# A fused delta rule and rational MoE on one core: the second layer's products one unit later, with a fourth operand buffer

## The chip, the cores and the metric

The kernel runs on one core of one Trainium2 chip. The metric is device time in microseconds (us). Engines in the text: PE is TensorE's matmul, PEld its weight load, DVE is VectorE, ACT is ScalarE, POOL is GpSimd, SP the engine whose queue issues nearly all DMAs.

## What is computed

A delta-rule attention over 768 steps for 4 x 8 heads of size 48 makes 3072 tokens of 384 values; a layer of 2048 hidden values with a rational activation follows.

```
for t in range(S):                       # attention, state is D x D per head
    y[:, :, t] = q_t @ state
    state = state + bt * outer(kt, vt - state @ kt)
x = y as [3072, 384]
h = x @ w_in                             # 384 x 2048
P = a[0] + a[1]*h + a[2]*h*h + a[3]*h*h*h
Q = 1 + |b[0]|*|h| + |b[1]|*h*h
out = (P / (Q + 1e-6)) @ w_out           # 2048 x 384
```

## The kernel before

The sequence is cut into 12 chunks of 64 steps (256 tokens each, all batches together). For each chunk the attention part is a chain: key products (`pg`), an inverse on DVE, query products (`pm`), a triangular solve in passes (`pu`, with the residuals `z_0`, `z_1`, `z_2`, `z`), the next state (`pd`, `S`), and the outputs `y` (line 788). `tokens(c)` turns `y` of a chunk into the layer's operand `xT`: a matmul and a DVE reduction find a scale (L806, L807), six PE transposes read `y` (L819), ACT copies the scale `sf` (L812), and ACT and DVE split the result into two fp16 halves (L246, L250).

The layer works in units: chunk c has 8 units j, each of 256 hidden values, written c.j below; there are 96. A unit has four steps:

- `hidden`: 18 matmuls into `ph` (L851).
- `numerator`: ACT makes `mu` and `mr` from `ph` (L868, L870), DVE does L871, L873, L875, ACT takes the absolute value `mw` (L874).
- `quotient`: ACT takes Ln and Exp (L886, L887); DVE makes the high half of the operand `mg` (L890 or L892), then L893; DVE (L897) or, in 4 of 8 units of chunks 2 to 10, POOL (L895) subtracts, and POOL makes the low half of `mg` (L898).
- `accumulate`: 12 matmuls of `mg` with `w_out` into the two banks `po` (L913), 6 for each bank. `po` is one pair of banks: the first unit of a chunk can write it only when ACT has moved the chunk before it out into the tile `ob` (L927, two copies, one for each bank), which then goes to memory.

Tiles with one tag share a fixed number of buffers, in the order in which the program asks for them. `mg` (and, while the weights are loaded, `wa` of `to_f32`) has MB = 3 buffers, as have `mu`, `mr` and `mw`. `ob` has one buffer, and the chunk's `y` has the same tag:

```
y = ys[c] = sb.tile([P, NPAIR, DM], F32, tag="ob", name=f"y_{c}", bufs=1)
obs[c] = sb.tile([P, NPAIR, DM], F32, tag="ob", name=f"ob_{c}", bufs=1)
```

In iteration n the program asks for numerator(n), quotient(n-1), the attention steps of position n+2, accumulate(n-2) and hidden(n+1). In chunk c's turn the attention part runs `back(c+1)`: `outputs` (which makes y of chunk c+1) at position 4, `tokens` (which reads it) at position 6, so at n = 8c+2 and n = 8c+4. A scheduler in the build then fixes the order of the instructions of each engine; each engine runs its list in that order.

Of the kernel before, what the change touches and what calls it, by code (L numbers as in the profile page):

```python
# [10 lines left out]
F16 = mybir.dt.float16  # L11
F32 = mybir.dt.float32
# [26 lines left out]
def kernel(  # L39
# [12 lines left out]
    nc = tc.nc  # L52
# [3 lines left out]
    P = 128  # L56
# [11 lines left out]
    NG = NPAIR * NH  # L68
    TG = NPAIR * P
    MB = 3  # L70
    SHIFT = 2
    SHAPE = {
        "k": [P, NPAIR, 2, NH, 2, C, HG],
# [9 lines left out]
    sb = ctx.enter_context(tc.tile_pool(name="sb", bufs=2))  # L83
# [282 lines left out]

    STAGES = (("mw", MB), ("mu", MB), ("mr", MB))
    stage = [0]

    def staged(shape, dtype, nm):  # L370
        stage[0] += 1
        tag, bufs = STAGES[stage[0] % len(STAGES)]
        return sb.tile(shape, dtype, tag=tag, name=nm, bufs=bufs)
# [4 lines left out]
    def to_f32(t, src, nm, keep=MIN_NORMAL):  # L378

        n = t.shape[-1]  # L380
        st = staged([P, n, 2], U32, "ws" + nm)
        nc.sync.dma_start(out=st.rearrange("p f w -> p (f w)"), in_=src)
        wl, wh = st[..., 0], st[..., 1]
        a = sb.tile([P, n], F32, tag="mg", name="wa" + nm, bufs=MB)
        nc.scalar.activation(a, wh.bitcast(F32), AF.Abs)
        nc.gpsimd.tensor_scalar(a, a, 3.0e38, keep, op0=ALU.min, op1=ALU.max)
        nc.vector.tensor_scalar(
            t, a.bitcast(U32), 3, KEEP, op0=ALU.logical_shift_left, op1=ALU.bitwise_and
        )
        for word, scalar, in1, op0, op1 in (  # L390
            (wh, 0xC0000000, t, ALU.bitwise_and, ALU.bitwise_or),
            (wl, 29, t, ALU.logical_shift_right, ALU.bitwise_or),
        ):
            nc.vector.scalar_tensor_tensor(out=t, in0=word, scalar=scalar, in1=in1, op0=op0, op1=op1)  # L394
# [428 lines left out]
    def scalars(c, lo, hi):  # L823

        d = toks[c]
        u = slice(lo, hi)
        sf = d["sf"]
        if c == 0:
            sf = sb.tile([P, 6], F32, tag="sf", name=f"sf_{c}_{lo}", bufs=3)
            pl = ps_h.tile([P, 6], F32, tag="h", name=f"pl_{c}_{lo}")  # L830
            looked_up(pl, d["hot"], t_x[:, int(lo > 0)])
            nc.scalar.copy(sf, pl)
        if lo == 0:
            d["m"] = sb.tile([P, 6, NU], F32, tag="msc", name=f"msc_{c}")
        nc.vector.tensor_mul(d["m"][:, :, u], tab[:, :, u], sf.unsqueeze(2).broadcast_to([P, 6, hi - lo]))
        d["ikap"][lo] = hi, sf[:, 1:2]
# [6 lines left out]
    def hidden(n):  # L843
        c, f2 = divmod(n, NU)
        x = toks[c]["x"]
        ph = ps_h.tile([P, 2, TG], F32, tag="h", name=f"ph_{n}")
        for i in range(2):
            k = 0
            for cc in range(NCC):
                for wp, xp in PASSES:  # L850
                    nc.tensor.matmul(  # L851
                        ph[:, i],
                        w_in[:, f2, wp, cc, i * P : (i + 1) * P],
                        x[:, xp, cc],
                        start=k == 0,
                        stop=k == 3 * NCC - 1,
                    )
                    k += 1
        unit[n] = {"ph": ph}

    def numerator(n):

        c, f2 = divmod(n, NU)
        d = unit[n]
        A3, B1, A1, B0, A0, Q0 = (toks[c]["m"][:, i, f2 : f2 + 1] for i in range(6))
        ph = d.pop("ph")
        u = sb.tile([P, 2, TG], F32, tag="mu", name=f"mu{n}", bufs=MB)
        nc.scalar.activation(u, ph, AF.Identity, scale=A3, bias=a2)  # L868
        r = z = sb.tile([P, 2, TG], F32, tag="mr", name=f"mr{n}", bufs=MB)
        nc.scalar.activation(z, ph, AF.Abs, scale=B1)  # L870
        nc.vector.tensor_mul(u, ph, u)  # L871
        w = sb.tile([P, 2, TG], F32, tag="mw", name=f"mw{n}", bufs=MB)
        nc.vector.scalar_tensor_tensor(out=w, in0=z, scalar=B0, in1=ph, op0=ALU.add, op1=ALU.mult)  # L873
        nc.scalar.activation(w, w, AF.Abs)  # L874
        nc.vector.scalar_tensor_tensor(out=u, in0=u, scalar=A1, in1=ph, op0=ALU.add, op1=ALU.mult)  # L875

        by_pool = 2 <= c < NCH - 1 and f2 in (0, 4, 5, 6)
        if by_pool:
            nc.gpsimd.tensor_scalar(u, u, A0, 1.0, op0=ALU.add, op1=ALU.mult)  # L879
        d.update(u=u, w=w, r=r, A0=A0, Q0=Q0, by_pool=by_pool)  # L880

    def quotient(n):

        d = unit[n]
        u, w, r, A0, Q0, by_pool = (d.pop(x) for x in ("u", "w", "r", "A0", "Q0", "by_pool"))
        nc.scalar.activation(r, w, AF.Ln, bias=Q0)  # L886
        nc.scalar.activation(r, r, AF.Exp, scale=-1.0)  # L887
        g = sb.tile([P, 2, 2, TG], F16, tag="mg", name=f"mg{n}", bufs=MB)
        if by_pool:
            nc.vector.tensor_mul(g[:, 0], u, r)  # L890
        else:
            nc.vector.scalar_tensor_tensor(out=g[:, 0], in0=u, scalar=A0, in1=r, op0=ALU.add, op1=ALU.mult)  # L892
        nc.vector.scalar_tensor_tensor(out=w, in0=w, scalar=Q0, in1=g[:, 0], op0=ALU.add, op1=ALU.mult)  # L893
        if by_pool:
            nc.gpsimd.tensor_sub(u, u, w)  # L895
        else:
            nc.vector.scalar_tensor_tensor(out=u, in0=u, scalar=A0, in1=w, op0=ALU.add, op1=ALU.subtract)  # L897
        nc.gpsimd.tensor_mul(g[:, 1], u, r)  # L898
        d["g"] = g

    def accumulate(n):
        c, f2 = divmod(n, NU)
        g = unit.pop(n)["g"]
        lo = max(i for i in toks[c]["ikap"] if i <= f2)
        hi, ikap = toks[c]["ikap"][lo]
        if f2 == lo:
            acc[c] = [ps_o.tile([P, DM], F32, tag=f"o{p}", name=f"po_{c}_{lo}_{p}") for p in PAIRS]
        po = acc[c]

        for k, (gp, wp) in enumerate(sorted(PASSES)):  # L910
            for i in range(2):
                for p in PAIRS:
                    nc.tensor.matmul(  # L913
                        po[p],
                        g[:, gp, i, p * P : (p + 1) * P],
                        w_out[:, f2, wp, i],
                        start=f2 == lo and i == 0 and k == 0,
                        stop=f2 == hi - 1 and i == 1 and k == len(PASSES) - 1,
                    )
        if f2 < hi - 1:  # L920
            return
        if lo == 0:
            obs[c] = sb.tile([P, NPAIR, DM], F32, tag="ob", name=f"ob_{c}", bufs=1)
        ob = obs[c]
        for p in PAIRS:
            if lo == 0:
                nc.scalar.activation(ob[:, p], po[p], AF.Copy, scale=ikap)  # L927
            else:
                nc.vector.scalar_tensor_tensor(
                    out=ob[:, p], in0=po[p], scalar=ikap, in1=ob[:, p], op0=ALU.mult, op1=ALU.add  # L930
                )
        if hi == NU:
            for b in range(2):
                dst = out[2 * b * S : (2 * b + 2) * S].rearrange("(p t) e -> t p e", p=NPAIR)
                nc.sync.dma_start(out=dst[c * C : (c + 1) * C], in_=ob[b * C : (b + 1) * C])
# [74 lines left out]
    def attention(c, j):  # L1010
        for f, cc in ((back, c + 1), (middle, c + 2), (front, c + 3), (ahead, c + 4)):
            if cc < NCH:
                f(cc, j)
# [16 lines left out]
    for what in ORDER:  # L1030
# [15 lines left out]
        f2 += what == "a"  # L1046
    for j in range(SHIFT):
        attention(0, j)
    N = NCH * NU
    hidden(0)  # L1050
    for n in range(N + 2):
        c, j = divmod(n, NU)
        if n < N:
            numerator(n)
        if 0 <= n - 1 < N:
            quotient(n - 1)
        attention(*divmod(n + SHIFT, NU))
        if 0 <= n - 2 < N:
            accumulate(n - 2)
        if n == GRP - 1 and GRP < NU:  # L1060
            tables(GRP, NU)
            scalars(0, GRP, NU)
        if n + 1 < N:
            hidden(n + 1)
# [26 lines left out]
```

## Time and profile before

| | |
|---|---|
| median of 3 runs | 855.29 us (854.32, 855.29, 863.12) |
| the profiled execution | 859.42 us, of it 857.2 us span |
| busy: DVE, PE, ACT, POOL | 760.8, 622.0, 544.9, 482.7 us |
| granted TensorE clock | 0.886 mean |

Busy time is a sum over the span. The span has three parts: weights are loaded until 147 us, attention and units run together until about 770 us, and the last chunk's units end it. Waits are told with the engine and tile that ended them.

### The profile page before, as it was taken

How to read it: one execution, taken by the hardware profiler on the slowest of the kernel's cores; microseconds unless marked ns; L12 is line 12 of the kernel's file. 1: busy time of each engine (PE TensorE's matmuls, PEld its weight loads, DVE VectorE, ACT ScalarE, POOL GpSimd, SP SyncE). 2: the span in 40 equal slices, each digit the busy share in tenths (PEclk: the TensorE clock that was granted, in tenths of full speed). 3: DMA queues.
4: the chain of work that ended last, by engine and by line, in shares of the span. 5: the costliest groups of instructions: out<-in, count | busy, mean ns of one | idle time of the engine just before them, and what ended most of it. 6: DMA issues, size and time to landing. Idle time of an engine off the chain costs nothing.

```text
span 857.2 us, 22995 instructions
## 1 busy us (share of the span) xinstructions
PE 622.0 (73%) x9290; PEld 492.0 (57%) x9290; DVE 760.8 (89%) x1312; ACT 544.9 (64%) x980; POOL 482.7 (56%) x452
## 2 busy tenths in 40 slices
PE   0220344766878688878798697995987989999895
PEld 0220344546666475666586585774775767777663
DVE  5998799697989969989989968999789999898996
ACT  4766656645666465677586574766566766677774
POOL 7655666355326437646736864766665635454532
PEclk9755555897988989989999899998989999999999
DMA  8996868898787875965997988598778672500000
GB/s 235 247 205 132 191 160 152 152 159 152 141 142 130 154 147 89 176 116 104 186 151 132 151 137 173 90 167 150 123 151 153 94 151 47 102 2 20 1 20 19
DMA packets 466506, 111.46 MB, mean 130 GB/s; under 512 B 431328, under 2 KB 463072, under 8 KB 466400
## 3 DMA queue, kind: packets, MB, share of 16 engines
q1 hardware_dynamic: 464224, 108.83, 67.8%
q8 instruction: 73, 1.20, 0.6%
q10 hardware_dynamic: 2176, 1.17, 0.5%
q14 instruction: 33, 0.27, 0.1%
HBM read 40.47 MB, written 26.23 MB: 78 GB/s over the span
## 4 chain that ended last, share of the span: by engine, by line
DVE 40%; DMA 16%; PE 14%; ACT 9%; issue 9%; SPq 7%; POOL 4%; POOLq 0%; ACTq 0%; DVEq 0%
PE ph L851 4%; PE po L913 4%; DVE mw L893 4%; DVE mw L873 3%; DVE mu L871 3%; DVE mg L892 3%; DVE mu L897 3%; DVE w_out L394 3%; DVE pr L636 2%; DVE mu L875 2%; DMA gd<-g 2%; DMA gb<-gd 2%; SPq L676 2%; POOL mg L898 2%; DMA wc<-img 1%
## 5 line engine op out<-in xcount | busy, mean ns | idle before, releaser
L913 PE MATMUL po<-w_out,mg 128*128 128x384 f16 x1152 | 224.9, 341 | 50.5 <-POOL mg L898 43.0
L851 PE MATMUL ph<-xT,w_in 128*128 128x256 f16 x1728 | 216.6, 278 | 13.1 <-DVE mu L875 11.4
L898 POOL TENSOR_TENSOR mg<-mu,mr 128x512 f16<-128x512 f32 x96 | 134.1, 1398 | 115.0 <-DVE mu L897 85.3
L851 PEld LDWEIGHTS <-w_in 128*128 128x128 f16 x1728 | 169.2, 100 | 45.5 <-issue 12.5
L913 PEld LDWEIGHTS <-mg 128*128 128x128 f16 x1152 | 110.2, 101 | 126.5 <-POOL mg L898 51.3
L868 ACT ACTIVATE mu<-ph,coef,msc 128x512 f32<-128x512 f32 x96 | 74.0, 771 | 45.5 <-POOL mg L898 31.0
L874 ACT ACTIVATE mw<-mw 128x512 f32<-128x512 f32 x96 | 60.3, 628 | 64.4 <-DVE mw L873 64.1
L893 DVE SCALAR_TENSOR_TENSOR mw<-mw,msc,mg 128x512 f32<-128x512 f32 x96 | 96.1, 1002 | 0.5
L470 PEld LDWEIGHTS <-kbd 128*128 128x128 f16 x1680 | 61.9, 105 | 36.4 <-issue 27.8
L871 DVE TENSOR_TENSOR mu<-ph,mu 128x512 f32<-128x512 f32 x96 | 65.4, 681 | 19.1 <-ACT mr L870 16.5
L875 DVE SCALAR_TENSOR_TENSOR mu<-mu,msc,ph 128x512 f32<-128x512 f32 x96 | 70.7, 736 | 0.0
L873 DVE SCALAR_TENSOR_TENSOR mw<-mr,msc,ph 128x512 f32<-128x512 f32 x96 | 70.5, 735 | 0.0
L886 ACT ACTIVATE mr<-mw,msc 128x512 f32<-128x512 f32 x96 | 69.2, 720 | 1.5
L895 POOL TENSOR_TENSOR mu<-mu,mw 128x512 f32<-128x512 f32 x36 | 48.7, 1353 | 32.8 <-DVE mw L893 29.1
L870 ACT ACTIVATE mr<-ph,msc 128x512 f32<-128x512 f32 x96 | 65.3, 680 | 0.0
L470 PE MATMUL pu<-z,ebd 128*128 128x48 f16 x1728 | 53.3, 187 | 15.7 <-DVE z L250 14.2
L470 PEld LDWEIGHTS <-ebd 128*128 128x128 f16 x1728 | 52.6, 99 | 19.5 <-issue 16.8
L887 ACT ACTIVATE mr<-mr 128x512 f32<-128x512 f32 x96 | 60.3, 628 | 1.4
L892 DVE SCALAR_TENSOR_TENSOR mg<-mu,msc,mr 128x512 f16<-128x512 f32 x60 | 56.9, 949 | 4.3 <-ACT mr L887 4.3
L879 POOL TENSOR_SCALAR mu<-mu,msc 128x512 f32<-128x512 f32 x36 | 34.2, 949 | 38.8 <-DVE mu L875 38.7
L897 DVE SCALAR_TENSOR_TENSOR mu<-mu,msc,mw 128x512 f32<-128x512 f32 x60 | 54.3, 907 | 0.4
L470 PEld LDWEIGHTS <-wbd 128*128 128x128 f16 x1152 | 35.1, 99 | 33.9 <-issue 30.4
(211 smaller groups left out, 1247.8 us busy)
## 6 DMA issues: line engine op xcount, KB each, us to landing
wsi<-in_moe_w_in_dram SPq DMA_DIRECT2D x24, 256.0 KB, 5.2
xdk<-kn SPq DMA_DIRECT2D x24, 256.0 KB, 3.9
kbd<-tk SPq DMA_DIRECT2D x24, 256.0 KB, 4.5
gd<-g SPq DMA_DIRECT2D x24, 256.0 KB, 4.3
wso<-in_moe_w_out_dram SPq DMA_DIRECT2D x32, 192.0 KB, 4.3
xdq<-kn SPq DMA_DIRECT2D x24, 256.0 KB, 4.3
mbd<-mm SPq DMA_DIRECT2D x24, 256.0 KB, 5.0
wc<-img SPq DMA_DIRECT2D x24, 256.0 KB, 5.1
```

What stands on the lines that cost most here:

```text
L470: nc.tensor.matmul(dst[p][:, h], head(bd, lp, p * H + h), head(rt, rp, p * H + h), start=start and n == 0 and h == 0, stop=stop and n == l ...
L851: nc.tensor.matmul(ph[:, i], w_in[:, f2, wp, cc, i * P : (i + 1) * P], x[:, xp, cc], start=k == 0, stop=k == 3 * NCC - 1,)
L868: nc.scalar.activation(u, ph, AF.Identity, scale=A3, bias=a2)
L871: nc.vector.tensor_mul(u, ph, u)
L873: nc.vector.scalar_tensor_tensor(out=w, in0=z, scalar=B0, in1=ph, op0=ALU.add, op1=ALU.mult)
L875: nc.vector.scalar_tensor_tensor(out=u, in0=u, scalar=A1, in1=ph, op0=ALU.add, op1=ALU.mult)
L886: nc.scalar.activation(r, w, AF.Ln, bias=Q0)
L892: nc.vector.scalar_tensor_tensor(out=g[:, 0], in0=u, scalar=A0, in1=r, op0=ALU.add, op1=ALU.mult)
L893: nc.vector.scalar_tensor_tensor(out=w, in0=w, scalar=Q0, in1=g[:, 0], op0=ALU.add, op1=ALU.mult)
L897: nc.vector.scalar_tensor_tensor(out=u, in0=u, scalar=A0, in1=w, op0=ALU.add, op1=ALU.subtract)
L898: nc.gpsimd.tensor_mul(g[:, 1], u, r)
L913: nc.tensor.matmul(po[p], g[:, gp, i, p * P : (p + 1) * P], w_out[:, f2, wp, i], start=f2 == lo and i == 0 and k == 0, stop=f2 == hi - 1 a ...
```

## The change

The loop takes accumulate(n-3) in place of accumulate(n-2), and runs one iteration more; the tag `mg` has four buffers in place of three, in the weight load too. The last line reserves less on-chip memory for DMA.

```
+    LAG = 3
...
-        a = sb.tile([P, n], F32, tag="mg", name="wa" + nm, bufs=MB)
+        a = sb.tile([P, n], F32, tag="mg", name="wa" + nm, bufs=MB + 1)
...
-        g = sb.tile([P, 2, 2, TG], F16, tag="mg", name=f"mg{n}", bufs=MB)
+        g = sb.tile([P, 2, 2, TG], F16, tag="mg", name=f"mg{n}", bufs=MB + 1)
...
-    for n in range(N + 2):
+    for n in range(N + LAG):
...
-        if 0 <= n - 2 < N:
-            accumulate(n - 2)
+        if 0 <= n - LAG < N:
+            accumulate(n - LAG)
...
-    nc = _bacc.Bacc("TRN2", target_bir_lowering=False, num_devices=1)
+    nc = _bacc.Bacc("TRN2", target_bir_lowering=False, num_devices=1, dynamic_dma_scratch_size=1024)
```

The scheduler's lists differ in many places. Line numbers of the changed kernel are higher by one (L928 is L927 of before). The following places lie in the turn of chunk 4.

First ACT. Before, the two copies that move chunk 3 out of `po` (L927) stand ahead of the copy that makes `y` of chunk 5 (L788):

```order
L927 ACTIVATE ob_7013<-po_0_0_6126,sf_5203 128x384
L927 ACTIVATE ob_7013<-po_0_1_6127,sf_5203 128x384
L561 ACTIVATE sq_6982<-k_6466 128x768
L868 ACTIVATE mu_7037<-ph_7018,coef,msc_6358 128x512
L870 ACTIVATE mr_7039<-ph_7018,msc_6358 128x512
L874 ACTIVATE mw_6789<-mw_6789 128x512
L246 ACTIVATE sh_7265<-S_149,sc_5652 128x768
L886 ACTIVATE mr_6786<-mw_6789,msc_6358 128x512
L565 ACTIVATE nrm_6981<-nrm_6981 128x16
L887 ACTIVATE mr_6786<-mr_6786 128x512
L566 ACTIVATE nrm_6981<-nrm_6981,consts 128x16
L788 ACTIVATE y_7203<-py_7106,sc_4562 128x768
```

Now `y` of chunk 5 (L789) stands 30 rows ahead of them, and the copies come between the scale `sf` of chunk 5's tokens (L813) and its `xT`:

```order
L247 ACTIVATE z_2_7878<-pu_7491,zmask 128x768
L813 COPY sf_7371<-px_7373 128x6
L875 ACTIVATE mw_7479<-mw_7479 128x512
L928 ACTIVATE ob_7211<-po_0_0_6228,sf_5191 128x384
L928 ACTIVATE ob_7211<-po_0_1_6229,sf_5191 128x384
L247 ACTIVATE xT_7368<-px_7373,sf_7371 128x768
L887 ACTIVATE mr_7476<-mw_7479,msc_6346 128x512
```

The two tiles have changed their turn in the one buffer: at n = 8c+2 the program asks for `y` of chunk c+1, then, in the same iteration, for `ob` of chunk c-1; with accumulate(n-2) it had asked for that `ob` one iteration earlier. This holds for c = 2 to 10. In chunk 1's turn `ob` of chunk 0 has been asked for at its fourth unit already, ahead of `y`.

Then PE at the transposes of the same `y`. Before, they follow products of the last unit 4.7 (`mg_7759`):

```order
L913 MATMUL po_0_0_7216<-w_out,mg_7759 128x384
L913 LDWEIGHTS mg_7759
L913 MATMUL po_0_1_7217<-w_out,mg_7759 128x384
L819 MATMUL px_7385<-identf,y_7203 128x128 x6
L470 LDWEIGHTS knbd_135
L470 MATMUL pd_8146<-z_8143,knbd_135 128x48
```

Now the first product of the chunk's first unit 4.0 (`mg_6783`) follows them; behind it stand 5 more of that unit for the first bank, 15 of units 4.1 to 4.3 for the first bank, and only then 4.0's 6 for the second bank:

```order
L279 LDWEIGHTS hx_7370
L279 MATMUL px_7373<-t_x,hx_7370 128x6
L820 MATMUL px_7373<-identf,y_7186 128x128 x6
L914 LDWEIGHTS mg_6783
L914 MATMUL po_0_0_7318<-w_out,mg_6783 128x384
```

Last DVE, around the scale of chunk 5's tokens. Before, the rows make the operand of units 4.6 (`mg_7603`) and 4.7 (`mg_7759`) here:

```order
L890 TENSOR_TENSOR mg_7603<-mu_7486,mr_7488 128x512
L871 TENSOR_TENSOR mu_7592<-ph_7573,mu_7592 128x512
L873 SCALAR_TENSOR_TENSOR mw_7597<-mr_7594,msc_6358,ph_7573 128x512
L647 TENSOR_SCALAR wh_7209<-wt_127 128x256
L250 SCALAR_TENSOR_TENSOR z_2_7890<-pu_7503,zmask,z_2_7890 128x768
L807 TENSOR_REDUCE xs_7381<-px_7385 128x1
L893 SCALAR_TENSOR_TENSOR mw_7491<-mw_7491,msc_6358,mg_7603 128x512
L875 SCALAR_TENSOR_TENSOR mu_7592<-mu_7592,msc_6358,ph_7573 128x512
L648 SCALAR_TENSOR_TENSOR wh_7209<-wt_127,wh_7209 128x256
L272 TENSOR_SCALAR xs_7381<-xs_7381 128x1
L562 TENSOR_REDUCE nrm_8071<-sq_8072 128x16
L892 SCALAR_TENSOR_TENSOR mg_7759<-mu_7592,msc_6358,mr_7594 128x512
```

Now those of 4.4 to 4.6 (`mg_7431`, `mg_7486`, and `mg_7591` a few rows on) come behind `xT`, one after the other:

```order
L276 TENSOR_SCALAR hx_7370<-xs_7369,key 128x1
L872 TENSOR_TENSOR mu_7474<-ph_7455,mu_7474 128x512
L874 SCALAR_TENSOR_TENSOR mw_7479<-mr_7476,msc_6346,ph_7455 128x512
L876 SCALAR_TENSOR_TENSOR mu_7474<-mu_7474,msc_6346,ph_7455 128x512
L251 SCALAR_TENSOR_TENSOR z_2_7878<-pu_7491,zmask,z_2_7878 128x768
L836 TENSOR_TENSOR msc_7436<-tab,sf_7371 128x48
L251 SCALAR_TENSOR_TENSOR xT_7368<-px_7373,sf_7371,xT_7368 128x768
L891 TENSOR_TENSOR mg_7431<-mu_7351,mr_7353 128x512
L894 SCALAR_TENSOR_TENSOR mw_7356<-mw_7356,msc_6346,mg_7431 128x512
L891 TENSOR_TENSOR mg_7486<-mu_7419,mr_7421 128x512
L894 SCALAR_TENSOR_TENSOR mw_7424<-mw_7424,msc_6346,mg_7486 128x512
```

With four buffers held by units 4.0 to 4.3, the operand of 4.4 has none until the 12 products of 4.0 are done.

## The prediction, made before the run

> **What bounds the kernel now.** I read the page's busy times first, then the three stages of the span as windows, then the waits. The columns of a window are its length, then the busy time of PE, PEld, DVE, ACT and POOL.
>
> ```profile
> PE 622.0 (73%) x9290; PEld 492.0 (57%) x9290; DVE 760.8 (89%) x1312; ACT 544.9 (64%) x980; POOL 482.7 (56%) x452
> ...
> 306.60:672.50 365.90, 303.31 (x4903) 242.49 (x4902) 328.66 (x493) 242.89 (x404) 225.59 (x184) 0.94 0.78 140
> 672.50:857.20 184.70, 162.34 (x2030) 124.11 (x2026) 165.64 (x238) 127.03 (x204) 86.19 (x67) 0.99 0.27 51
> ```
>
> DVE is busy 328.7 of 365.9 us (90%) where attention and units run together, with 37 us idle in six chunks, and 165.6 of 184.7 us afterwards. So DVE sets the pace, and an edit counts by the DVE idle time that it takes away or adds. The waits over the whole span (total us, times, longest) show who waits for the operand `mg`:
>
> ```profile
> POOL mg L898 <- DVE mu L897: 85.3, 30, 7.4
> PEld L913 <- POOL mg L898: 51.3, 33, 6.1
> PE po L913 <- POOL mg L898: 43.0, 28, 5.7
> ```
>
> PE's 43.0 us before the second layer are what the lag aims at. PE is not the bound, though; they count only where hidden(n+1), queued behind that product on PE, comes too late for DVE. DVE's own list of waits tells how much that is:
>
> ```profile
> DVE mu L871 <- ACT mr L870: 16.5, 12, 3.8
> ...
> DVE xT L250 <- ACT xT L246: 5.8, 5, 2.2
> ...
> DVE m L725 <- PE pm L470: 4.3, 3, 2.3
> ...
> DVE ab L615 <- DMA gb<-gd: 4.1, 5, 2.1
> ```
>
> L871 is the first DVE step of a numerator; it waits for ACT, and ACT for `ph`. The four largest of these waits in the stage of both parts are at the beginning of a chunk, when `hidden` has just received the new `xT`:
>
> ```profile
> 375.87 0.69 DVE L871 TENSOR_TENSOR mu<-ph,mu 128x512 f32<-128x512 f32 x1 [2.25 <-ACT mr L870]
> 435.03 0.69 DVE L871 TENSOR_TENSOR mu<-ph,mu 128x512 f32<-128x512 f32 x1 [2.37 <-ACT mr L870]
> ...
> 497.46 1.02 DVE L250 SCALAR_TENSOR_TENSOR xT<-px,sf,xT 128x768 f16<-128x768 f32 x1 [1.77 <-ACT xT L246]
> ...
> 503.39 0.69 DVE L871 TENSOR_TENSOR mu<-ph,mu 128x512 f32<-128x512 f32 x1 [1.97 <-ACT mr L870]
> ...
> 622.84 0.69 DVE L871 TENSOR_TENSOR mu<-ph,mu 128x512 f32<-128x512 f32 x1 [3.83 <-ACT mr L870]
> ```
>
> **The change part by part.** No compute instruction is added or taken away; the edits change order and waits only.
>
> *The one buffer of `y` and `ob`.* This is the step that I hold to decide. Before, chunk 3 leaves `po` well ahead of `y`, and the transposes that read `y` of chunk 5 come when the products of chunk 4 are all but finished:
>
> ```profile
> 440.42 1.06 ACT L927 ACTIVATE ob<-po,sf 128x384 f32<-128x384 f32 x2
> ...
> 447.57 0.88 ACT L788 ACTIVATE y<-py,sc 128x768 f32<-128x768 f32 x1
> ...
> 492.72 3.11 PE L913 MATMUL po<-w_out,mg 128*128 128x384 f16 x11
> 495.67 0.82 PE L819 MATMUL px<-identf,y 128*128 128x128 f32 x6
> ```
>
> From `ob` at 440.4 to the transposes at 495.7 are 55 us in which PE works on chunk 4's products. With the new turn, `ob` of chunk 3 has to wait until those transposes have read `y` of chunk 5. No product of chunk 4 can start earlier; units 4.0 to 4.3 fill the four buffers, and the quotients of 4.4 onward wait. So the fourth buffer adds no freedom here: a chunk's products are bunched behind the transposes.
>
> *What DVE waits there.* The clock begins when DVE has finished `z_1`, the solve's second residual. Durations, from the timeline and the chain (start, us), from the list of the tile `z` (min/median/max ns) and from the page's groups (busy us, mean ns, then idle time before):
>
> ```profile
> 496.32 1.37 PE L470 MATMUL pd<-z,knbd 128*128 128x48 f16 x48
> ...
> 388.86 2.12 PE po L913 x12
> ...
> L246 ACT ACTIVATE z<-pu,zmask x36: 880/901/907, 103.3 to 767.1; 128x768 f16<-128x768 f32 x36
> L250 DVE SCALAR_TENSOR_TENSOR z<-pu,zmask,z x36: 998/1006/1020, 106.1 to 768.1; 128x768 f16<-128x768 f32 x36
> ...
> L874 ACT ACTIVATE mw<-mw 128x512 f32<-128x512 f32 x96 | 60.3, 628 | 64.4 <-DVE mw L873 64.1
> ...
> L871 DVE TENSOR_TENSOR mu<-ph,mu 128x512 f32<-128x512 f32 x96 | 65.4, 681 | 19.1 <-ACT mr L870 16.5
> L875 DVE SCALAR_TENSOR_TENSOR mu<-mu,msc,ph 128x512 f32<-128x512 f32 x96 | 70.7, 736 | 0.0
> L873 DVE SCALAR_TENSOR_TENSOR mw<-mr,msc,ph 128x512 f32<-128x512 f32 x96 | 70.5, 735 | 0.0
> ```
>
> The chain follows the new rows: a solve pass of 48 matmuls on PE (1.4 us; `pd` has the same 48), ACT's `z` (0.9), the small copy `sf` (an estimate of 0.2), `mw` (0.6), the first of the two `ob` copies (1.06 for both, so about 0.5), then 27 products on PE until unit 4.0 is through with both banks: 27 x 2.12/12 = 4.8 us. Together 8.4 us. The transposes (0.8) lie beside ACT's part. DVE has, in the same rows, the small scale steps and `msc` (0.5), numerator 4.6 (0.68 + 0.74 + 0.74 = 2.15), `z_2` (1.0) and `xT` (1.0): 4.7 us. It idles 3.7 us in three pieces. The solve pass queued on PE behind these products is late by as much, but the `z` that needs it stands on DVE behind two quotients.
>
> Six turns (c = 2 to 7) have about this order, though in turns 2 and 3 the DVE rows hold less work of units or ACT has more ahead of `ob`. In turn 8 another numerator stands behind `xT`: I take half. In 9 and 10 two numerators stand there, enough to hide it: nothing. Sum 6 x 3.7 + 1.9 = **24 us added**. Bounds: 0, if DVE's list turns out to have work in each wait, and 9 x 7.4 = 67, if the wait is twice as long in all nine.
>
> *What goes.* While DVE catches up on the quotients c.4 to c.7, PE and ACT make the first hidden tiles of chunk c+1, so the wait at a chunk's beginning should vanish: 2.25 + 2.37 + 1.97 + 3.83 = 10.4 us, and the `xT` wait of 1.77, which is now part of the chain: **12 us removed**, bounds 5 and 17.
>
> *DVE beside POOL.* A quotient's DVE steps are slowed where POOL works (the list of a line, the timeline, the page's groups):
>
> ```profile
> L893 DVE SCALAR_TENSOR_TENSOR mw<-mw,msc,mg x96: 658/747/2201, 165.8 to 847.4; 128x512 f32<-128x512 f32 x96
> ...
> 486.85 2.05 DVE L893 SCALAR_TENSOR_TENSOR mw<-mw,msc,mg 128x512 f32<-128x512 f32 x1
> ...
> 486.00 2.36 POOL L248 TENSOR_TENSOR mm<-m,mm 128x1024 f16<-128x1024 f32 x1 [0.95 <-ACT mm L244]
> ...
> L893 DVE SCALAR_TENSOR_TENSOR mw<-mw,msc,mg 128x512 f32<-128x512 f32 x96 | 96.1, 1002 | 0.5
> ...
> L895 POOL TENSOR_TENSOR mu<-mu,mw 128x512 f32<-128x512 f32 x36 | 48.7, 1353 | 32.8 <-DVE mw L893 29.1
> ```
>
> For L893 the median is 0.75 us, the mean 1.00; the one at 486.85 lasts until shortly after POOL's `mm` ends at 488.36. In the new rows three quotients stand in a row, and POOL's subtraction and product for the first run just beside the second and third. If each of their four DVE steps pays 0.65 instead of the mean 0.25 us, that is 1.6 per turn and 11 us for seven; I take half of it, **6 us**. Bounds -6 (POOL's work leaves other places) and +18. [...]
>
> *The weight load.* Its `wa` tiles get the fourth buffer as well. ACT waits there for DVE to free one, and DVE once for POOL:
>
> ```profile
> ACT wao L385 <- DVE w_out L387: 6.2, 7, 2.1
> ...
> ACT wai L385 <- DVE w_out L387: 5.2, 5, 2.6
> ...
> DVE w_out L387 <- POOL wai L386: 4.7, 1, 4.7
> ```
>
> Only the last is DVE's: I take **2 us off**, bounds 0 and 5.
>
> *The scratch for DMA and the added iteration.* All DMAs of the profile's list are issued by SP or ACT, none by POOL, and the smaller reserve costs nothing. The last iteration adds no instruction; the last product waits for the same `mg`. SP's list is reordered too: DVE's waits that end on the DMA chain, `m` and `ab`, are 8.4 us in all, and the inverse now comes earlier against the units while the query products have more DVE work ahead of them. I take 0, bounds -8 and +8.
>
> *Sum.* The profiled execution took 859.4 us: 859.4 + 24 - 12 + 6 - 2 = 875.4. The median of the runs is 4.1 us below that execution, so the forecast is **871 us**.
>
> **Rivals.**
>
> *The backlog covers the wait (not slower).* The mechanism is DVE's list at the transposes: if SP's and PE's timing on the chip brings `xT` and the `ob` copies so early that DVE still has numerators 4.5 and 4.6 (4.3 us) to do, the wait shrinks from 3.7 to about 1.5 us. It decides at the chain's 8.4 us against DVE's work: with 7 us of work it is 1.4. For this speaks that DVE is 90% busy, against it that the rows put only one numerator there. Time: 7 x 1.5 = 10 in place of 24, and no contention: 859.4 + 10 - 12 - 2 - 4.1 = 851.
>
> *The lag pays as meant (faster).* Products never hold up `hidden`, DVE's waits at chunk beginnings go (12), those on `m` and `ab` too (8.4), and the weight load gives 4.7: 859.4 - 25 - 4.1 = 830; half of that is 842. It needs `ob` to be free in time, which the new order of `y` and `ob` speaks against. [...]
>
> *Each chunk loses its whole second half (much slower).* If the transposes come no earlier than now, the quotients that were done before them (in chunk 4 nearly all, since the products at 492.72 use their results) move behind them, and DVE has nothing in their place:
>
> ```profile
> L890 DVE TENSOR_TENSOR mg<-mu,mr 128x512 f16<-128x512 f32 x36 | 30.1, 836 | 5.3 <-ACT mr L887 2.7 <-POOL mu L879 1.8 <-ACT nrm L565 0.8
> ```
>
> With L893's 1.00, four quotients of 0.84 + 1.00 us are 7.4 us; seven turns 52, less 12: 859.4 + 40 - 4.1 = 895. For it speaks that `px` shares its PSUM bank with `pm`, which waits for a DMA (4.3 us above); against it, that the scheduler has moved inverse work ahead.
>
> **How the numbers follow.** A change of under 1% (855.29 +- 8.6) is about what a measurement of this kernel can't tell from none. Chances: the forecast's case, 858 to 884, 0.46; the backlog's, 846 to 860, 0.26; the faster one 0.15; the much slower one 0.13. The range runs from 846 to 896: the low end cuts off the faster case, the high end adds the contention's upper bound and some of the third rival. From the same cases: below 846.7 0.15; within 1% the backlog's 0.26 and 0.06 of the forecast's low end, 0.32; slower 0.53.
>
> **What the new profile would show.** If I am right, each `ob` copy (L928) of chunks 1 to 9 comes right behind a group of transposes (L820), PE's first product of a chunk behind `ob`, and DVE has waits before L891 or L893, put down to PE's products, of some 2 to 4 us a chunk, while L872 no longer waits at a chunk's beginning. L894's mean rises above 1.00 us if POOL gets in the way. The prediction is wrong if DVE's idle time stays at 37 us in the stage of both parts, or if its waits move to the DMA chain (`m`, `ab`) and exceed 8 us.

## The result and the profile after

The kernel after takes **894.6 us** (median of 4 runs, 891.1 to 897.1), the kernel before 855.4 in the same series: ratio 1.0435, 95% interval 1.0365 to 1.0505, 39 us slower. The prediction was 871 us, range 846 to 896. Its sign holds; the rise is two and a half times the one forecast. The profiled execution took 895.1 us with a span of 893.4 us.

Busy times of the page of after, then the three stages as windows (length, then busy PE, PEld, DVE, ACT, POOL; the last three columns are PE's granted clock, the DMA share and GB/s). The stages begin at the first `hidden` product of chunks 0, 2 and 8, as those of before did.

```profile
PE 634.9 (71%) x9290; PEld 499.6 (56%) x9290; DVE 768.5 (86%) x1312; ACT 543.8 (61%) x980; POOL 478.6 (54%) x452
```

```profile
141.60:289.40 147.80, 114.71 (x1761) 89.96 (x1761) 135.51 (x234) 86.36 (x146) 73.18 (x63) 0.89 0.86 152
289.40:699.70 410.30, 315.86 (x4941) 251.29 (x4939) 341.78 (x496) 242.83 (x404) 225.81 (x186) 0.90 0.72 127
699.70:893.40 193.70, 165.95 (x1988) 125.09 (x1986) 167.02 (x236) 128.59 (x205) 86.14 (x67) 0.98 0.24 46
```

DVE is busy 7.7 us longer than before (768.5 against 760.8) and idle 28.5 us longer (124.9 against 96.4). The middle stage holds most of it: chunks 2 to 7 take 410.3 in place of 365.9 us, with 68.5 us of DVE idle in place of 37.2 and DVE busy 13.1 us longer. The last stage is 9 us longer (193.7 against 184.7); what lies ahead of chunk 2 is 17 us shorter (289.4 against 306.6).

What the change aimed at did happen. In the page's group of PE's second-layer products the idle time put down to POOL's `mg` falls from 43.0 us to 13.4:

```profile
L914 PE MATMUL po<-w_out,mg 128*128 128x384 f16 x1152 | 208.6, 332 | 16.7 <-POOL mg L899 13.4
L894 DVE SCALAR_TENSOR_TENSOR mw<-mw,msc,mg 128x512 f32<-128x512 f32 x96 | 100.8, 1054 | 1.2
```

But DVE's own waits (total us, times, longest) now contain entries that follow PE and ACT at the turn of a chunk:

```profile
DVE mu L872 <- ACT mr L871: 19.0, 13, 3.7
DVE mg L891 <- PE po L914: 11.6, 6, 4.0
DVE z L251 <- ACT z L247: 9.5, 5, 4.7
DVE z L249 <- ACT z L245: 9.4, 2, 4.9
DVE xT L251 <- ACT xT L247: 9.4, 7, 2.8
...
DVE m L726 <- PE pm L471: 7.0, 4, 3.8
...
DVE w_out L388 <- POOL wai L387: 4.7, 1, 4.7
```

This is turn 4 in the timeline of after, engine by engine (start, us, the row, in brackets the idle time before it and what ended it):

```profile
479.95 1.27 POOL L899 TENSOR_TENSOR mg<-mu,mr 128x512 f16<-128x512 f32 x1
...
481.26 0.78 ACT L869 ACTIVATE mu<-ph,coef,msc 128x512 f32<-128x512 f32 x1 [1.01 <-POOL mg L899]
...
482.51 0.90 ACT L247 ACTIVATE z<-pu,zmask 128x768 f16<-128x768 f32 x1
483.29 0.17 ACT L813 COPY sf<-px 128x6 f32<-128x6 f32 x1
484.10 0.63 ACT L875 ACTIVATE mw<-mw 128x512 f32<-128x512 f32 x1 [0.64 <-DVE mw L874]
484.63 1.03 ACT L928 ACTIVATE ob<-po,sf 128x384 f32<-128x384 f32 x2
...
489.62 0.84 ACT L259 ACTIVATE sq<-q 128x768 f32<-128x768 f32 x1 [2.55 <-DMA q<-in_q_dram]
...
490.47 0.62 ACT L888 ACTIVATE mr<-mr 128x512 f32<-128x512 f32 x1
...
483.51 0.87 PE L820 MATMUL px<-identf,y 128*128 128x128 f32 x6 [2.72 <-ACT sf L813]
485.25 6.23 PE L914 MATMUL po<-w_out,mg 128*128 128x384 f16 x27 [0.86 <-ACT ob L928]
...
478.35 1.02 DVE L251 SCALAR_TENSOR_TENSOR z<-pu,zmask,z 128x768 f16<-128x768 f32 x1 [0.81 <-ACT z L247]
...
482.72 0.69 DVE L872 TENSOR_TENSOR mu<-ph,mu 128x512 f32<-128x512 f32 x1 [3.04 <-ACT mr L871]
...
486.50 1.02 DVE L251 SCALAR_TENSOR_TENSOR xT<-px,sf,xT 128x768 f16<-128x768 f32 x1 [0.73 <-ACT xT L247]
491.52 0.69 DVE L891 TENSOR_TENSOR mg<-mu,mr 128x512 f16<-128x512 f32 x1 [4.00 <-PE po L914]
```

Transposes of `y`, `ob`, then the chunk's products in one bunch: the order that the prediction read from the rows. DVE waits three times here, 7.8 us in all. In turns 3 and 5 the last wait stands in another place, at the solve's third residual:

```profile
424.26 0.96 DVE L249 TENSOR_TENSOR z<-pu,z 128x768 f16<-128x768 f32 x1 [4.85 <-ACT z L245]
...
558.87 0.96 DVE L249 TENSOR_TENSOR z<-pu,z 128x768 f16<-128x768 f32 x1 [4.53 <-ACT z L245]
...
422.61 0.85 ACT L259 ACTIVATE sq<-q 128x768 f32<-128x768 f32 x1 [4.25 <-DMA q<-in_q_dram]
...
423.45 0.78 ACT L245 CAST z<-pu 128x768 f16<-128x768 f32 x1
...
416.13 1.32 PE L471 MATMUL pu<-z,ebd 128*128 128x48 f16 x46
```

ACT's part of that residual (L245) stands behind a square of the newly loaded `q`, and ACT waits for the load. PE's solve pass that feeds it (the last row) ends at 417.5, just as the products begin.

### The profile page after: what moved, and what is told of

The parts are those of the page before. It is cut to its first block, busy times and chain, and to the rows that moved or that the text cites. A ratio compares the mean times of both kernels' runs of the same rounds, so it can differ in the third digit from the quotient of the medians.

```text
span 893.4 us, 23004 instructions
## 1 busy us (share of the span) xinstructions
PE 634.9 (71%) x9290; PEld 499.6 (56%) x9290; DVE 768.5 (86%) x1312; ACT 543.8 (61%) x980; POOL 478.6 (54%) x452
## 5 line engine op out<-in xcount | busy, mean ns | idle before, releaser
L852 PE MATMUL ph<-xT,w_in 128*128 128x256 f16 x1728 | 229.9, 291 | 55.6 <-DVE mu L876 52.0
L852 PEld LDWEIGHTS <-w_in 128*128 128x128 f16 x1728 | 174.9, 104 | 94.6 <-DVE mu L876 34.8
L914 PE MATMUL po<-w_out,mg 128*128 128x384 f16 x1152 | 208.6, 332 | 16.7 <-POOL mg L899 13.4
L914 PEld LDWEIGHTS <-mg 128*128 128x128 f16 x1152 | 110.5, 100 | 88.7 <-POOL mg L899 18.0
L894 DVE SCALAR_TENSOR_TENSOR mw<-mw,msc,mg 128x512 f32<-128x512 f32 x96 | 100.8, 1054 | 1.2
L869 ACT ACTIVATE mu<-ph,coef,msc 128x512 f32<-128x512 f32 x96 | 74.1, 772 | 42.2 <-POOL mg L899 26.5
L872 DVE TENSOR_TENSOR mu<-ph,mu 128x512 f32<-128x512 f32 x96 | 65.5, 683 | 27.8 <-ACT mr L871 19.0
L471 PEld LDWEIGHTS <-kbd 128*128 128x128 f16 x1680 | 63.2, 104 | 28.8 <-issue 24.3
L896 POOL TENSOR_TENSOR mu<-mu,mw 128x512 f32<-128x512 f32 x36 | 51.1, 1423 | 47.0 <-DVE mw L894 41.4
L471 PE MATMUL pu<-z,ebd 128*128 128x48 f16 x1728 | 57.3, 188 | 15.3 <-DVE z L251 15.2
L893 DVE SCALAR_TENSOR_TENSOR mg<-mu,msc,mr 128x512 f16<-128x512 f32 x60 | 64.9, 1084 | 2.6 <-ACT mr L888 2.5
L471 PEld LDWEIGHTS <-ebd 128*128 128x128 f16 x1728 | 55.5, 99 | 19.8 <-issue 16.9
L871 ACT ACTIVATE mr<-ph,msc 128x512 f32<-128x512 f32 x96 | 65.3, 680 | 0.0
L471 PEld LDWEIGHTS <-wbd 128*128 128x128 f16 x1152 | 37.5, 102 | 49.1 <-issue 48.4
L880 POOL TENSOR_SCALAR mu<-mu,msc 128x512 f32<-128x512 f32 x36 | 28.7, 798 | 52.0 <-DVE mu L876 50.3
L898 DVE SCALAR_TENSOR_TENSOR mu<-mu,msc,mw 128x512 f32<-128x512 f32 x60 | 50.3, 838 | 0.5
```

What stands on the lines that cost most here:

```text
L471: nc.tensor.matmul(dst[p][:, h], head(bd, lp, p * H + h), head(rt, rp, p * H + h), start=start and n == 0 and h == 0, stop=stop and n == l ...
L852: nc.tensor.matmul(ph[:, i], w_in[:, f2, wp, cc, i * P : (i + 1) * P], x[:, xp, cc], start=k == 0, stop=k == 3 * NCC - 1,)
L914: nc.tensor.matmul(po[p], g[:, gp, i, p * P : (p + 1) * P], w_out[:, f2, wp, i], start=f2 == lo and i == 0 and k == 0, stop=f2 == hi - 1 a ...
```

## The experiments

**Is it the turn of `y` and `ob`?** Three kernels. The first is after with a buffer of its own for `y`; the second after with accumulate ahead of attention in the loop, which puts `ob` ahead of `y` again; the third is before (lag 2, three `mg` buffers) with `y`'s tile claimed one solve step earlier, so that only the turn changes.

```
own y:      - y = ys[c] = sb.tile([P, NPAIR, DM], F32, tag="ob", ...)
            + y = ys[c] = sb.tile([P, NPAIR, DM], F32, tag="yo", ...)
acc first:  the line attention(*divmod(n + SHIFT, NU)) moved behind accumulate(n - LAG)
turn alone: (before, in back(c, 3))
            + ys[c] = sb.tile([P, NPAIR, DM], F32, tag="ob", ...)
            + nc.gpsimd.memset(ys[c][:, 0, 0:1], 0.0)
```

> The changed kernel with a tag and a buffer of its own for y, so that ob never waits for it; lag, fourth buffer and the place of accumulate stay. T: 835 to 855 us, like the run with accumulate ahead of attention. L: 885 to 900 us.

> The changed kernel with one thing undone: in the loop accumulate(n-3) stands ahead of the attention steps, so that ob of chunk c-1 takes the one shared buffer ahead of y of chunk c+1 again; lag and fourth buffer stay. Theory T (the turn of y and ob costs the time): the 44 us lost in turns 2 to 7 go, what was gained ahead of chunk 2 (some 17 us) stays: 838 to 855 us. Rival L (the lag, or the scheduler's other reordering, costs it): 885 to 900 us.

> The kernel before (lag 2, three buffers) with the turn alone: the buffer of y is taken one position earlier, at the third solve step, by a memset of one column on POOL, so that y of chunk c+1 comes ahead of ob of chunk c-1. T: slower, and by more than the changed kernel's later turns, since only three operands fit and a fifth quotient per chunk is held back: 890 to 925 us. L: as before, 850 to 862 us.

Measured: own `y` 844.2 us (0.9911, 0.9875 to 0.9947); accumulate first 856.8 (1.0045, 1.0012 to 1.0079); the turn alone 894.2 (1.0490, 1.0460 to 1.0520). The turn alone makes the kernel before as slow as the kernel after, and taking it away, in either of two ways, takes the loss away (with accumulate first all but 4 us, 2 us above the range expected). The own buffer alone isn't what helps, as the next three show.

**What are the two intended edits worth?** After with lag 2 (the fourth buffer alone), after with three buffers (the lag alone, turned), and before with the own `y`.

```
lag2_buf4:  (after)  - LAG = 3          + LAG = 2
lag3_buf3:  (after)  - bufs=MB + 1      + bufs=MB       (both tiles with the tag mg)
lag2_own_y: (before) tag="ob" -> tag="yo" for y, DMA scratch 1024
```

> The changed kernel with LAG = 2: the fourth mg buffer alone, ob ahead of y as before. If the buffer gives the earlier beginning of chunks 0 to 2 (142, 216, 289 us against 147, 222, 307), this kernel has it too: 838 to 850 us. If it comes from the lag, or if the later turns give it back, as before: 850 to 860 us.

> The changed kernel with three mg buffers in place of four: lag 3 alone. T: the turn stays and one more quotient per chunk is held back behind the transposes, so slower than 894.6 us: 900 to 920. L: 890 to 898 us, since the lag is the same. If the fourth buffer in the weight load gave the early gain, chunk 2 begins later than at 289 us, at about 300.

> The kernel before (lag 2, three mg buffers) with a buffer of its own for y. In the kernel before, y waits for the way out of ob (ACT y <- DMA out 5.9 us), ACT only. Theory T: ob was already in time, so little to gain: 850 to 858 us; then the 10 us by which lag 3, four buffers and an own y beat the kernel before come from lag and buffer. Rival: the separate buffer itself gives them: 842 to 848 us.

Measured: 848.5 us (0.9941, 0.9921 to 0.9961), 890.2 (1.0445, 1.0406 to 1.0484) and 854.0 (1.0008, 0.9982 to 1.0035). The fourth buffer with the old lag gains 6 us; an own `y` alone gains nothing. The run with three buffers missed its expectation: with the turn it is no slower than with four. Without the turn, lag and buffer together gain 10 us (844.2).

**Why twice the wait?** From the end of DVE's step at 478.35 (479.4) to the freed buffer at 491.5 the chain of turn 4 takes 12.1 us, where the prediction had 8.4. Its rows name the surplus: ACT's numerator waits for POOL until 481.26 and delays `z`, `sf` and the transposes (1.7 us); `mw` waits for DVE (0.6); 27 products take 6.23 in place of 4.8 us (1.4). Two edits take the first and the last away: more buffers for the three tiles of a numerator, and one accumulator tile, so that products come unit by unit and 12 instead of 27 free the first `mg`.

```
mu4:    - u = ... tag="mu", bufs=MB       + bufs=MB + 1
three4: the same for mu, mr and mw
po_one: - acc[c] = [ps_o.tile([P, DM], F32, tag=f"o{p}", ...) for p in PAIRS]
        + acc[c] = ps_o.tile([P, NPAIR, 512], F32, tag="o", ...)
        - for p in PAIRS: nc.scalar.activation(ob[:, p], po[p], AF.Copy, scale=ikap)
        + nc.scalar.activation(ob, po[:, :, :DM], AF.Copy, scale=ikap)
```

> The changed kernel with a fourth buffer for mu. Theory M (numerator c.6, the work that DVE was to have in the wait, is itself held up, because mu's three buffers belong to c.3, c.4 and c.5 until POOL's product of c.3 is done, and z_2, sf, the transposes and ob stand behind it on ACT): the L872 waits of 3.0, 1.2, 2.8 and 2.8 us before the transposes in turns 4 to 7 go and the chain ends some 2 us earlier in each of six turns: 880 to 887 us. Rival (the solve passes and the 27 products set the chain's end, DVE only waits at another row): 891 to 898 us.

> Lag 3, four mg buffers, a buffer of its own for y (the 844 us version) and a fourth for mu. M says mu is short only behind the turn: 840 to 848 us. If mu holds up numerators everywhere (ACT mu <- POOL mg 31 us before), faster: 830 to 840 us.

> The kernel after with a fourth buffer for each of the three tiles mu, mr and mw, so that numerator c.6 need not wait until POOL has finished the product of unit c.3. Theory T1 (this wait is the first half of DVE's doubled wait in each turn): DVE's wait before the numerator behind the transposes, 2.3 to 3.0 us in each of six turns, goes, DVE's idle time in chunks 2 to 8 falls from 68 to about 54 us, time 876 to 884 us. Rival T2 (the numerator comes earlier, but what follows in the turn, the products behind ob, ends at the same time, so the wait only moves): 891 to 898 us, idle time 65 us or more.

> The kernel after with the two accumulators po of a chunk as one tile that one ACT step copies, so that PE takes the products unit by unit (12 products until the first mg buffer is free, where the kernel after has about 27, the first pair of all units ahead of the second). Theory T3 (the bunch of 27 products is the second half of the doubled wait): 15 products of 0.23 us less per turn, 3.5 us, in six turns 21 us: 870 to 878 us, and DVE's wait on po before L891 falls from 4.0 to about 1 us. Rival T2 (DVE has to wait for the whole bunch anyway, or for another link that ends as late): 889 to 898 us.

Measured: 906.0 us (1.0620, 1.0583 to 1.0658), 854.7 (1.0009, 0.9982 to 1.0035), 896.8 (1.0485, 1.0443 to 1.0527) and 889.4 (1.0406, 1.0368 to 1.0443). All expectations that the loss would shrink by a third or more missed, and the own `y` with a fourth `mu` missed both of its ranges. With one `po` tile DVE's longest wait on products before L891 fell from 4.0 to 2.2 us, not to 1. In the run with `mu` alone the third tile, `mr`, waited for the same POOL step (ACT idle 0.55 us before L871 at 484.96). In the windows of the other two (three4, then po_one) the middle stage did lose DVE idle time as its theory said, to 402.9 - 346.9 = 56.0 and 402.0 - 342.8 = 59.2 us, but other stages grew: with four buffers chunk 2 begins 8 us later, the last stage is 6 us longer and DVE's steps in the middle take 5 us more; with one tile the last stage is 3 us longer:

```profile
297.30:700.20 402.90, 319.75 (x4987) 257.79 (x4987) 346.92 (x499) 243.36 (x407) 228.26 (x186) 0.89 0.75 133
```

```profile
288.50:690.50 402.00, 318.00 (x4939) 253.94 (x4939) 342.83 (x495) 242.59 (x398) 223.24 (x186) 0.90 0.73 130
```

To tell the price of the turn from the edit's own cost, each edit was run without the turn too, and both together:

> The kernel after with four buffers each of mu, mr and mw, and y with a buffer of its own: the same as the earlier run with four buffers each (896.8 us), but without the turn of y and ob. The difference of the two is the price of the turn where the wait for POOL is away; in the kernel after it is 894.6 - 844.2 = 50 us. Theory T1 (the wait for POOL, 1.7 us in each turn by the timeline, is part of the price, and the edit cost elsewhere what it saved): price 32 to 40 us, this kernel 857 to 865 us. Rival T2 (that wait is no part of it, another link ends as late): price about 50 us, 843 to 850 us.

> The kernel after with one po tile of both accumulators, and y with a buffer of its own: the same as the earlier run with one po tile (889.4 us) without the turn. Theory T3 (the bunch of 27 products makes 15 x 0.23 = 3.5 us of each turn's wait): price of the turn 25 to 32 us, so this kernel 857 to 864 us, slower than with two tiles. Rival T2 (the bunch is no part of the price): price about 45 to 50 us, 840 to 845 us.

> The kernel after with four buffers each of mu, mr and mw and with one po tile. Theory T4 (both links lie on the chain and add): DVE's idle time in chunks 2 to 8, 68.5 us in the kernel after, 56 with the buffers alone and 59 with the one tile alone, falls to 45 to 50 us; time 882 to 888 us, with what the buffers cost in chunks 0 to 2 in it. Rival T2: idle time 56 us or more, 890 to 897 us.

> The same with both edits, and y with a buffer of its own. Theory T4: the price of the turn with both links away is 20 to 27 us, about the 24 us of the forecast, so this kernel takes about 860 us. Rival T2: the price stays 45 us or more, this kernel 840 to 850 us.

Measured: 853.2 us (0.9993, 0.9965 to 1.0022), 831.6 (0.9745, 0.9696 to 0.9793), 897.9 (1.0528, 1.0497 to 1.0559) and 857.4 (1.0048, 1.0029 to 1.0066). None of these supports a smaller price: by differences it is 43.5, 57.8 and 40.5 us (table below). The last link under suspicion was the buffers of `mg` themselves, with six and eight in place of four:

```
mg6, mg8: - bufs=MB + 1     + bufs=MB + 3, MB + 5     (both tiles with the tag mg)
```

> The kernel after with six buffers of mg in place of four, y and ob still turned. Theory B (DVE idles in the turn because the quotients c.4 onward find no free mg buffer, whatever the chain's single links are): two more quotients, 2 x 1.8 us of DVE work, fit into each wait of 7.4 us, six turns 21 us, so about 873 us (865 to 880). Rival C (the buffers don't decide, as the run with three buffers, 890 us, was no slower than that with four; the wait is the numerators' and xT's): 889 to 900 us.

> The kernel after with eight buffers of mg, one for each unit of a chunk, y and ob still turned. Theory B: all quotients of a chunk can come ahead of its products, the wait of DVE on products before L891 goes, DVE's idle time in chunks 2 to 8 falls from 68 to about 45 us, time 845 to 860 us. Rival C: 889 to 900 us.

> The same with eight buffers and y with a buffer of its own, so that nothing turns. Theory B: the turn costs under 15 us here, where it cost 40 to 58 with four buffers. Rival C: it still costs 40 to 58 us.

Measured: 895.8 us (1.0487, 1.0437 to 1.0537), 892.7 (1.0455, 1.0412 to 1.0497) and, without the turn, 856.1 (1.0009, 0.9969 to 1.0050). With eight buffers no wait of DVE before L891 is put down to products any more. Here are the middle and the last stage of that kernel, then of the same without the turn:

```profile
292.20:692.10 399.90, 316.76 (x4987) 253.68 (x4987) 352.40 (x508) 245.94 (x408) 231.60 (x189) 0.89 0.77 137
692.10:892.90 200.80, 169.74 (x2036) 128.11 (x2034) 163.76 (x233) 126.83 (x202) 87.02 (x65) 0.96 0.23 45
...
290.10:670.90 380.80, 310.10 (x4958) 246.81 (x4958) 333.82 (x499) 242.30 (x404) 226.72 (x187) 0.93 0.78 143
670.90:851.60 180.70, 162.42 (x2070) 125.09 (x2066) 161.05 (x237) 126.77 (x204) 86.69 (x66) 0.99 0.26 50
```

Theory B was right on the wait and wrong on the time. DVE's idle time in the middle stage fell from 68.5 to 47.5 us, as it expected, and is the same without the turn (47.0). But the stage is still 19 us longer with the turn than without, now because DVE is busy 18.6 us longer (with nine steps more in the window), and the last stage is 20 us longer, mostly with DVE idle. So the waits at the turn are a part of what the kernel after loses, but without them the loss is nearly as large, in other places.

All pairs together, the differences turned minus not turned (idle is span less busy time, from the profiled executions):

| setting | turned, us | not turned, us | price of the turn, us | DVE busy, us | DVE idle, us |
|---|---|---|---|---|---|
| before's lag and buffers | 894.2 | 854.0 | 40.2 | +8.8 | +35.5 |
| after | 894.6 | 844.2 | 50.4 | +16.0 | +30.0 |
| mu4 | 906.0 | 854.7 | 51.4 | +10.7 | +38.4 |
| three4 | 896.8 | 853.2 | 43.5 | +19.3 | +27.2 |
| po_one | 889.4 | 831.6 | 57.8 | +21.0 | +34.5 |
| three4 and po_one | 897.9 | 857.4 | 40.5 | +9.1 | +29.9 |
| mg8 | 892.7 | 856.1 | 36.6 | +14.8 | +26.5 |

The price is 37 to 58 us whichever link is taken away. So it isn't the length of one chain. One thing that the turned kernels share shows when PE's second-layer products are counted in the 20 us behind the transposes of turns 2 to 7. Each row is the sum of six such windows, 120 us: of before, of after, of after with the own `y`, of after with eight `mg` buffers, each of L914 (L913 in before) alone.

```profile
sum 120.00, PE 28.82 PEld 14.10; mean PE 4.80 PEld 2.35
```

```profile
sum 120.00, PE 75.26 PEld 40.03; mean PE 12.54 PEld 6.67
```

```profile
sum 120.00, PE 23.48 PEld 11.92; mean PE 3.91 PEld 1.99
```

```profile
sum 120.00, PE 73.98 PEld 39.91; mean PE 12.33 PEld 6.65
```

And all work of the same windows, of after and then of after with the own `y`:

```profile
sum 120.00, PE 112.81 PEld 81.14 DVE 83.83 ACT 69.85 POOL 67.66; mean PE 18.80 PEld 13.52 DVE 13.97 ACT 11.64 POOL 11.28
```

```profile
sum 120.00, PE 114.70 PEld 98.95 DVE 92.74 ACT 92.05 POOL 70.17; mean PE 19.12 PEld 16.49 DVE 15.46 ACT 15.34 POOL 11.70
```

PE is busy 94% and 96% of these stretches, so in both kernels it is all but full there. With the turn it spends 75.3 us of them on products, without it 23.5. The 51.8 us between are missing from the work that feeds ACT and DVE, as the rows of `hidden` (L852) and of the solve and inverse passes (L471) show. The first pair is `hidden` in after and in after with the own `y`, the second the passes in the same order:

```profile
sum 120.00, PE 17.03 PEld 14.85; mean PE 2.84 PEld 2.47
...
sum 120.00, PE 51.34 PEld 40.05; mean PE 8.56 PEld 6.68
```

```profile
sum 120.00, PE 30.26 PEld 28.28; mean PE 5.04 PEld 4.71
...
sum 120.00, PE 47.87 PEld 47.16; mean PE 7.98 PEld 7.86
```

`hidden` loses 34.3 us and the passes 17.6, together 51.9. With them ACT falls by 22 us and DVE by 9 us in the six stretches. Earlier in the chunk, while `ob` is awaited, PE has no products to do (in turn 4 none from 449.8 to 485.2 us). But 9 us are a small part of 50, and with eight `mg` buffers DVE is busy 92.9 us in its six stretches, as long as in after with the own `y` (92.7), though the turn costs 36.6 us there. A last run takes load off PE and leaves the program's order and its buffers:

```
- for k, (gp, wp) in enumerate(sorted(PASSES)):      (in accumulate)
+ for k, (gp, wp) in enumerate([(1, 0)]):
```

> The kernel after with only one of the three products of the second layer (low half of mg by the high half of w_out), 384 matmuls in place of 1152; the output lacks the other two parts. The order of y and ob, the buffers and the waits stay as in the kernel after. Theory P (the price of the turn is PE's: in the 20 us behind the transposes 12.3 us of products push aside what PE must give to DVE): the bunch is 4 us, the price falls to about a third, 850 to 866 us. Rival O (the price is a chain of waits by the order itself, whatever the load on PE): 880 us or more.

Measured: 853.0 us (0.9992, 0.9965 to 1.0019). Its page, and that of after with the own `y` for comparison:

```profile
PE 532.6 (63%) x8522; PEld 436.0 (51%) x8522; DVE 753.0 (89%) x1312; ACT 543.7 (64%) x980; POOL 478.7 (56%) x452
```

```profile
PE 625.5 (74%) x9290; PEld 495.3 (58%) x9290; DVE 752.5 (89%) x1312; ACT 542.2 (64%) x980; POOL 483.4 (57%) x452
```

With a third of the products DVE is busy 753.0 us and idle 94.2 (span 847.2), as without the turn (752.5 and 94.9), though the turn is there. In its six stretches PE is no longer full (94.2 of 120 us), the products take 25.3 us and the passes are back at 48.3. `hidden` is back to 29.2 us only, and DVE to 88.2 of the 92.7 us. The rows are all work, passes, products and `hidden`:

```profile
sum 120.00, PE 94.19 PEld 79.20 DVE 88.19 ACT 73.47 POOL 86.91; mean PE 15.70 PEld 13.20 DVE 14.70 ACT 12.25 POOL 14.48
...
sum 120.00, PE 48.29 PEld 46.57; mean PE 8.05 PEld 7.76
...
sum 120.00, PE 25.27 PEld 11.84; mean PE 4.21 PEld 1.97
...
sum 120.00, PE 29.15 PEld 22.36; mean PE 4.86 PEld 3.73
```

The time lies in theory P's range and outside rival O's. It isn't proof of P, for the totals agree only as a sum. Here are the middle and the last stage of the run, then of after with the own `y`:

```profile
283.60:654.10 370.50, 263.02 (x4545) 219.47 (x4545) 330.43 (x494) 242.58 (x402) 220.40 (x182) 0.89 0.78 140
654.10:847.20 193.10, 134.22 (x1756) 103.50 (x1751) 166.89 (x244) 129.80 (x207) 94.18 (x71) 0.90 0.27 52
...
283.20:663.80 380.60, 313.87 (x4900) 249.74 (x4899) 331.73 (x497) 241.51 (x403) 227.06 (x185) 0.91 0.77 139
663.80:847.40 183.60, 165.16 (x2075) 127.07 (x2074) 164.49 (x240) 129.81 (x207) 86.82 (x68) 0.97 0.28 52
```

The middle stage is 10 us shorter than without the turn, so there a part of what was won seems to be a gain from less work on PE, with or without the turn. The last stage is 9.5 us longer than without the turn and as long as in after (193.7), so there the turn's price stays although two thirds of the products are gone. The same cut without the turn wasn't run. That PE's load has a part in the price is therefore likely; how large a part is open.

## Why the prediction was right in its sign and wrong in its size

- **The turn of the buffer: right.** In the kernel after, `ob` of chunks 1 to 9 stands behind the transposes and the products behind `ob`, as in the rows of turn 4, and the kernel with the turn alone shows that this is the loss.
- **"What DVE waits there", 24 us: the step that failed.** In the timeline, from 6.1 us ahead of the end of the transposes to 13 us behind it and without the waits on `m`, DVE waits 5.5, 9.2, 10.1, 7.5, 6.2 and 6.0 us in turns 2 to 7, 7.4 on average where the prediction had 3.7, and 1.4 and 0.9 in turns 8 and 10: 46.7 us. Two things were put at nothing. First, links of the chain: in turn 4 it takes 12.1 in place of 8.4 us, by ACT's wait for POOL (1.7), the wait of `mw` for DVE (0.6) and slower products (1.4). Second, the third residual, because "the `z` that needs it stands on DVE behind two quotients". This holds in turns 2, 4, 6 and 7; in turns 3 and 5 `z` stands ahead of the quotients and waits 4.85 and 4.53 us, for ACT behind the load of `q`, and not for the products on PE.
- **These waits don't explain the price.** Counted alike (every wait over 0.5 us in these stretches of turns 2 to 7, those on `m` too), DVE waits 48.2 us in after, 16.8 in before and 26.7 in after with the own `y`. With eight `mg` buffers and the turn it is 19.4 us, and that kernel takes 892.7 us all the same. Nor does the load of `q`: ACT's waits for it are 25.6 us in after and 6.7 with eight buffers. The chain's links changed little when they were taken out. Why the turn costs 37 to 58 us, and not what DVE waits at the transposes, stays open; PE's load is the candidate that the last run speaks for.
- **"What goes", 12 us: right in place.** From chunk 3 to chunk 8 L872 no longer waits at a chunk's beginning; one wait of 3.74 us is new, 10 us into chunk 2. DVE's idle time rose by 28.5 us, 46.7 at the turns less some 18 elsewhere. The 18 us are that remainder and no sum of rows, so they confirm neither the 12 nor the 2 us.
- **DVE beside POOL, 6 us: near in number, by luck.** DVE is busy 7.7 us longer than before, but that is 13.1 us more in the middle stage, 1.4 more in the last and 6.8 less ahead of chunk 2. L894's mean rises from 1.00 to 1.05 us. The 0.65 us that a step was to pay was an estimate, which no run shows as such. In the timeline of before, 45 of 94 steps of L893 have POOL's work beside them for over 0.3 us and last 1.26 us on average; the other 49 last 0.75 us, none over 0.84. In the pairs the turn costs 9 to 21 us of longer DVE steps, and lag 3 without it shortens them (752.5 against 760.8), so the small net hides two larger parts.
- **The weight load, 2 us:** the wait named, L388 for POOL, is still there with 4.7 us; `hidden` of chunk 0 begins 5 us earlier all the same (141.6 against 147).
- **`m` and `ab`, 0 +- 8:** 7.0 + 1.1 against 4.3 + 4.1 us, right.
- **The rivals.** "Lag pays as meant" (830 to 842) is near what the two edits give once the turn is away: 844. "The backlog covers the wait" fell. The third rival's 895 us, and its 7.4 us a turn, were met. Its mechanism, quotients that are held back, would be cured by eight buffers: they took the idle time of the middle stage away and not the loss, so it isn't the whole of it either.

## What to carry to other kernels

When code moves in program order, look for tiles of different kinds that share one buffer, and ask whose turn it is now: here an edit meant for `mg` turned `y` and `ob`, and a buffer of 3 KB per partition (the own `y`) makes 50 us of difference. The waits that a trace shows at such a place are time lost in that kernel, but taking them away need not give it back: with eight `mg` buffers 21 us of idle time went and 2 us of time. So measure the pair, each variant with the turn and without it, before a link is called the cause. If no link changes the time, change the load, and run that change without the turn too. The version to keep is lag 3 with the fourth `mg` buffer, an own `y` and one accumulator tile, 831.6 us, 0.9745 (0.9696 to 0.9793) of before; why the one tile gains 13 us beside the own `y` is open.

## What was not expected of the hardware

The bunch of products ran slowly at first: 27 in 6.23 us, where 12 in 2.12 us make 4.8. The granted clock (the column behind POOL) of after is low just there, after PE's waits of 2.72 and 0.86 us:

```profile
484.00:488.00 4.00, 3.14 (x14) 1.56 (x13) 2.79 (x5) 2.97 (x5) 0.69 (x1) 0.70 1.36 184
488.00:492.00 4.00, 4.00 (x30) 2.35 (x29) 0.48 (x1) 2.29 (x5) 0.00 (x0) 0.87 0.93 175
```

In the next window, 492 to 496, the clock is 1.00. In turn 3, where the clock stays at 1.00, 48 products take 7.96 us. The 27 products of turn 4 took 1.4 us longer than the 4.8, with the clock at 0.70 and 0.87. Why it falls there isn't shown. The clock doesn't explain the loss: in the whole middle stage it is 0.90 in after and 0.94 in before, but 0.91 in after with the own `y`, which is 50 us faster.
